# Gated attention and MLP on one core: strict program order on every engine, scores in groups of three, u turned a chunk after loading, and a new first batch

## The chip, the cores and the metric

One core of a Trainium2 chip runs the kernel. The metric is the device time of one execution in microseconds (us); lower is better. The kernel before takes 1306.66 us (median of 3 runs, 1306.63 to 1307.92).

## The reference

```python
def attn(u, v, z):                       # u, v: (8, 3008, 256), z: (8, 3008, 64)
    scores = (1.0 / S) * z @ z.transpose(0, 2, 1)
    return u * (np.maximum(scores, 0.0) ** 2 @ v)

def moe(x, w_in, w_out):                 # x: (24064, 256), w_in: (256, 2048), w_out: (2048, 256)
    h = x @ w_in
    return (h / (1.0 + np.exp(-1.702 * h))) @ w_out
# out = moe(attn(u, v, z).reshape(24064, 256), w_in, w_out)
```

Scores are symmetric, so the kernel computes only the upper half of the score blocks and gets the lower half by DMA transposes.

## The kernel before

A batch has 3008 rows, in six chunks of 512 (the last has 448). Each batch goes through attention (chunks 0 to 5), then up-projections (`up_group`, 48 of them, a tile `hg` each) and down-projections (`down`, halves of 128 rows, tile `yp`). Scores (`sc`) of a chunk pair are made in groups, ahead of their use; ScalarE rectifies (`rl`), VectorE squares (`a`), SyncE issues the DMA transposes (`tt`). The parts that matter:

```python
    ps2 = ctx.enter_context(tc.tile_pool(name="ps2", bufs=3, space=bass.MemoryType.PSUM))  # sc and hg share these
    ps1 = ctx.enter_context(tc.tile_pool(name="ps1", bufs=2, space=bass.MemoryType.PSUM))  # o and yp share these
    ctx.enter_context(tc.manual_schedule(engines={mybir.EngineType.PE}))  # the rest: ordered by a scheduler
    # ... cut ...
    def load_u(b, i):                    # 4 DMAs on SyncE's queue, then the transpose on VectorE
        # ... cut: uq <- u, two buffers ...
        dve.transpose(ut[...], uq[...])
    # ... cut ...
    def scores(b, group, dve_relu=False):
        # ... cut: two half-height matmuls for each sc ...
            act.activation(rl, sc, AF.Relu, scale=csc)
            dve.tensor_tensor(a, rl, rl, ALU.mult)
            # ... cut: one or two sp.dma_start_transpose(t, a) ...
    # ... cut ...
        def gate(c):                     # frees the accumulator acc[c]
            dve.tensor_tensor(x[:, c, :n], acc[c][:, :n], ut[:, :n], ALU.mult)
    # ... cut ...
    LEAD = {30: 2, 36: 2, 42: 2}         # score groups of the next batch among the up-projections
    TAIL = {2: 3, 5: 3}                  # and among the last down-projections
    # ... cut ...
    for b in range(B):
        for i in range(NCH):
            if i + 1 < NCH:
                load_u(b, i + 1)
            for n, step in enumerate(attend(b, i, both=(b == 0 and i == 0))):
                take(b, sched[i].get(n, 0))          # a score group
                if i == NCH - 1 and n % 5 == 2 and h < HEAD:
                    up_group(b, h); h += 1
                step()                               # a matmul of V with a
            if b == 0 and i == 1:
                # ... cut: pool.dma_start of W1 (4 DMAs) and W2 ...
        # ... cut: load_z, load_v, load_u of the next batch ...
        for q in range(HEAD, nup):
            take(b + 1, LEAD.get(q, 0))
            up_group(b, q)
            if q >= LAGY:
                down(b, *downs.pop(0))
        for n in range(len(downs)):
            take(b + 1, TAIL.get(n, 0), dve_relu=True)
            down(b, *downs[n])
```

Of the kernel before, what the change touches and what calls it, by code (L numbers as in the profile page):

```python
# [9 lines left out]
F32 = mybir.dt.float32  # L10
F16 = mybir.dt.float16
P = 128
# [3 lines left out]
def kernel(  # L16
# [51 lines left out]
    ctx.enter_context(tc.manual_schedule(engines={mybir.EngineType.PE}))  # L68

    ident = const.tile([P, P], F16, name="ident")  # L70
    make_identity(nc, ident)

    ZT, V16, UT, XT, unit, TT = {}, {}, {}, {}, {}, {}

    def warm_up(n):

        nil = const.tile([P, CH], F16, name="nil")
        dve.memset(nil, 0.0)
        w = ps1.tile([P, CH], F32, name="w", tag="ps1")
        for k in range(n):  # L80
            pe.matmul(w, nil[:, :P], nil, start=(k == 0), stop=(k == n - 1))

    def first_z(g):

        if g == 0:
            ZT[0] = pz.tile([P, NJ, P], F16, name="ZT", tag="ZT")
            ZT["st"] = pz.tile([P, NJ, 2, DQK], F16, name="zst", tag="zst")
        if g % CB == 0:
            ZT["f"] = pw.tile([P, CB, CB, DQK], F32, name="zf", tag="y")
        n0 = g * CB  # L90
        zf = ZT["f"][:, g % CB]
        full = min(CB, NJ - 1 - n0)
        sp.dma_start(zf[:, :full, :], z[0, n0 * P:(n0 + full) * P].rearrange("(n p) d -> p n d", p=P))
        if full < CB:
            for h in range(2):
                sp.dma_start(zf[h * SREM:(h + 1) * SREM, full, :], z[0, S0:S])
        z2 = ZT["st"][:, n0:n0 + CB]
        for c in range(2):
            dve.tensor_copy(z2[:, :, c, :], zf)
        return z2  # L100

    def first_zt(g, z2):
        zp = ps1.tile([P, CB, P], F16, name="zp", tag="ps1")
        for k in range(CB):
            pe.transpose(zp[:, k, :], z2[:, k, :, :], ident)
        act.activation(ZT[0][:, g * CB:(g + 1) * CB, :], zp, AF.Copy, scale=1.0)  # L106
# [14 lines left out]
    def load_v(b, eng):  # L121


        V16[b] = pz.tile([P, NJ, NCC, P], F16, name="V16", tag="V16")
        for n0 in range(0, NJ, VB):
            vst = pu.tile([P, VB, D], F32, name="vst", tag="vst", bufs=3)
            full = min(VB, NJ - 1 - n0)
            eng.dma_start(vst[:, :full, :], v[b, n0 * P:(n0 + full) * P].rearrange("(n p) c -> p n c", p=P))
            if full < VB:
                for h in range(2):  # L130
                    eng.dma_start(vst[h * SREM:(h + 1) * SREM, full, :], v[b, S0:S])
            for k in range(NCC):
                pool.tensor_copy(
                    V16[b][:, n0:n0 + VB, k, :].rearrange("p n (q c) -> p n q c", c=QW),
                    vst.rearrange("p n (q k c) -> p n q k c", k=NCC, c=QW)[:, :, :, k, :],
                )
# [4 lines left out]
    def load_u(b, i):  # L141
        n = width(i)
        uq = pu.tile([P, CH // QW, NCC, QW], F32, name="uq", tag="uq")
        src = u[b, i * CH:i * CH + n].rearrange("(q t) c -> t q c", t=QW)
        for k in range(P // QW):
            cs = slice(k * NCC * QW, (k + 1) * NCC * QW)
            sp.dma_start(uq[k * QW:(k + 1) * QW, :n // QW].rearrange("t q k c -> t q (k c)"), src[:, :, cs])  # L147
        ut = pu.tile([P, NCC, CH // QW, QW], F32, name="ut", tag="ut")
        UT[b, i] = ut
        dve.transpose(ut[:, :, :n // QW, :].rearrange("p k q t -> p q k t"), uq[:, :n // QW])  # L150


    def scores(b, group, dve_relu=False):
# [11 lines left out]
        for n, ((i, jp), sc) in enumerate(zip(group, scs)):  # L165
            rl = pw.tile([P, 2, CH], F16, name="rl", tag="rl", bufs=5)
            if dve_relu and n == 2:
                dve.tensor_scalar(rl, sc, 0.0, csc, ALU.max, ALU.mult)
            else:
                act.activation(rl, sc, AF.Relu, scale=csc)  # L170
            a = pa.tile([P, 2, CH], F16, name="a", tag="a", bufs=21)
            unit[b, i, jp] = a
            dve.tensor_tensor(a, rl, rl, ALU.mult)  # L173
            cj = jp // 2
            if cj > i:
                if (b, i, cj) not in TT:
                    TT[b, i, cj] = pa.tile([P, CB, CB, P], F16, name="tt", tag="tt", bufs=14)
                t = TT[b, i, cj]
                k0 = 2 * (jp % 2)
                if cj < NCH - 1:  # L180
                    sp.dma_start_transpose(
                        t[:, k0:k0 + 2].rearrange("p r g c -> p (r g) c"),
                        a.rearrange("p r c -> p (r c)"),
                    )
                else:
                    for r in range(2):
                        sp.dma_start_transpose(t[:, :, k0 + r, :], a[:, r, :])  # L187
# [12 lines left out]
    def attend(b, i, both=False):  # L200


        n = width(i)
        acc = {}

        def open_(c):
            if c not in acc:
                acc[c] = ps1.tile([P, CH], F32, name="o", tag="ps1")
                return True
            return False  # L210

        def mm(c, j):
            new = open_(c)
            last = c == 1 and j == NJ - 2 and not both
            pe.matmul(acc[c][:, :n], V16[b][:, j, c, :], weights(b, i, j), start=new, stop=last)  # L215
            if last:
                gate(c)

        def half():
            a = unit[b, i, NU - 1][:, 1, :n]  # L220
            for c in range(2):
                h = slice(c * SREM, (c + 1) * SREM)
                new = open_(c)
                pe.matmul(acc[c][:, :n], V16[b][h, NJ - 1, c, :], a[h], start=new, stop=not new)  # L224
            for c in range(2 if both else 1):
                gate(c)
# [13 lines left out]
        js = range(NJ - 1)  # L240
        if both:
            return [lambda j=j, c=c: mm(c, j) for j in js for c in range(2)] + [half]
        return [lambda j=j: mm(0, j) for j in js] + [half] + [lambda j=j: mm(1, j) for j in js]


# [27 lines left out]
    def down(b, k, s, h):  # L273
# [15 lines left out]
        if h == 1 and s == ns - 1:  # L289
            r0 = b * S + i * CH  # L290
            full = min(n, S - i * CH) // P
            act.dma_start(
                out[r0:r0 + full * P].rearrange("(n p) c -> p n c", p=P), Y[b, k][:, :full, :],
            )
            if full < ns:
                for h_, bb in enumerate((b, b - 1)):
                    act.dma_start(
                        out[bb * S + S0:(bb + 1) * S], Y[b, k][h_ * SREM:(h_ + 1) * SREM, full, :],
                    )


    LAGY = NFG + 1
    HEAD = 9

    def pieces(i):
        return [(i, jp) for jp in range(2 * i, NU)]

    def split(lst, sizes):
# [9 lines left out]

    LEAD = {30: 2, 36: 2, 42: 2}
    TAIL = {2: 3, 5: 3}  # L320
    SCHED = {
        0: {8: 3, 15: 2, 23: 3, 34: 2},
        1: {6: 3, 23: 3, 34: 2},
        2: {8: 3, 23: 3},
        3: {8: 2, 23: 2},
        4: {23: 2},
        5: {},
    }

    SCHED0 = {  # L330
        0: {0: 2, 8: 2, 16: 2, 24: 2, 32: 3, 40: 3},
        1: {0: 2, 8: 2, 15: 3, 23: 3, 34: 2},
        2: SCHED[2], 3: SCHED[3], 4: SCHED[4], 5: {},
# [4 lines left out]
    def take(b, n, **kw):  # L338
        if n:
            group = [queue.pop(0) for _ in range(n)]  # L340
            scores(b, group, **kw)
# [5 lines left out]
    warm_up(12)  # L347
    fill(0)
    z2 = [first_z(g) for g in range(NCH)]
    load_v(0, act)  # L350
    load_u(0, 0)
    first_zt(0, z2[0])
    take(0, 2)
    first_zt(1, z2[1])
    take(0, 2)
    for g in range(2, NCH):
        first_zt(g, z2[g])

    for b in range(B):
        nup = NCH * NFG  # L360
        sched = SCHED if b else SCHED0
        for i in range(NCH):
            if i + 1 < NCH:
                load_u(b, i + 1)
            h = 0
            for n, step in enumerate(attend(b, i, both=(b == 0 and i == 0))):
                take(b, sched[i].get(n, 0))
                if i == NCH - 1 and n % 5 == 2 and h < HEAD:
                    up_group(b, h)
                    h += 1  # L370
                step()
            if b == 0 and i == 1:
                w1v = moe_w_in.rearrange("(q k c) f -> q c k f", k=NCC, c=QW)
# [4 lines left out]
        if more:  # L378
            load_z(b + 1)
            load_v(b + 1, sp)  # L380
            load_u(b + 1, 0)
            fill(b + 1)
        downs = down_list(b)
        for q in range(HEAD, nup):
            if more:
                take(b + 1, LEAD.get(q, 0))
# [3 lines left out]
        for n in range(len(downs)):  # L390
            if more:
                take(b + 1, TAIL.get(n, 0), dve_relu=True)
# [31 lines left out]
```

## Time and profile before

| | before |
|---|---|
| time, median | 1306.66 us |
| span of the profiled run | 1304.2 us |
| TensorE busy | 96% |
| first relu; first V matmul | 15.26 us; 22.8 us |
| V matmuls of chunk 1 begin | 47.9 us |
| V matmuls of batch 1 begin | 200.5 us |

The last three rows are read from the timeline. Below is the top of the profile page of the kernel before: span, busy time, granted clock by fortieths of the span (in tenths of full speed), and the chain of waits that ended last. In the profile PE is TensorE, PEld its weight loads, DVE VectorE, ACT ScalarE, POOL GpSimd and SP SyncE; a q after the name is that engine's instruction queue, and L with a number a line of that run's own kernel.

```profile
span 1304.2 us, 19129 instructions
PE 1249.4 (96%) x7556; PEld 682.2 (52%) x7556; DVE 823.0 (63%) x899; ACT 748.7 (57%) x810; POOL 96.4 (7%) x149
PEclk7899999999999999999999999999999999999999
...
PE 88%; DMA 4%; DVE 3%; ACT 3%; issue 1%; SPq 1%; ACTq 0%; DVEq 0%
```

TensorE is the bottleneck; idle time of any other engine costs nothing until it makes TensorE wait. Next, the table of waits of the kernel before (who waited for whom: total us, times, longest).

```profile
DVE ut L150 <- DMA uq<-in_u_dram: 27.9, 5, 9.9
...
PE hg L259 <- DVE gt L268: 13.4, 14, 1.0
...
PE sc L160 <- ACT ZT L106: 9.9, 2, 9.2
...
PE o L215 <- DVE a L173: 7.6, 2, 6.4
...
PE hg L259 <- ACT rl L170: 6.3, 7, 0.9
```

The two `hg` lines are one stop of about 1 us for each of the 21 score groups among the up-projections. One of them in the timeline (start, length, engine, line, operation, count, idle time before and its releaser):

```profile
158.34 0.60 PE L160 MATMUL sc<-ZT 64*128 64x512 f16 x4
158.63 1.23 DVE L268 TENSOR_TENSOR gt<-hg,sg 128x1024 f16<-128x1024 f32 x1 [0.51 <-ACT sg L267]
158.77 1.94 ACT L170 ACTIVATE rl<-sc 128x1024 f16<-128x1024 f32 x2 [0.18 <-PE sc L160]
...
159.91 1.02 PE L259 MATMUL hg<-xt,W_58 128*128 128x512 f16 x4 [0.96 <-DVE gt L268]
```

Two score tiles and the previous `hg` hold all three two-bank PSUM buffers, so the next up-projection waits until the product `gt` has freed one.

### The profile page before, as it was taken

To read this page: it belongs to the slowest core of one execution; us is meant where nothing else is said; L and a number is where in the kernel's file an instruction comes from. 1 tells how busy PE (TensorE), PEld (TensorE's weight loads), DVE (VectorE), ACT (ScalarE), POOL (GpSimd) and SP (SyncE) were. 2 spreads that over 40 slices of the span, in tenths; PEclk is the share of its full clock that TensorE was granted. 3 is DMA by queue.
4 is the path that set the end of the run, shared out by engine and by line. 5 is a ranking of instruction groups with operands and counts; after the bars stand their busy time and mean duration, and the time that the engine had idled before them with its cause. 6 is when DMAs were issued, how large, how long until landed. Compare 5 with 4: busy or idle time off the path is not lost.

```text
span 1304.2 us, 19129 instructions
## 1 busy us (share of the span) xinstructions
PE 1249.4 (96%) x7556; PEld 682.2 (52%) x7556; DVE 823.0 (63%) x899; ACT 748.7 (57%) x810; POOL 96.4 (7%) x149
## 2 busy tenths in 40 slices
PE   5789999999999999999999999999999999999998
PEld 2235664456634566346653465544655456644566
DVE  3436767477754776657766577656776567664674
ACT  4525666356663676536765367644676446663564
POOL 5002000030000200012000120002100010000000
PEclk7899999999999999999999999999999999999999
DMA  9979348791387916894157842678437742285011
GB/s 198 161 148 197 85 116 158 149 173 46 81 166 135 167 34 113 148 149 134 50 119 152 128 136 63 124 146 126 133 66 142 135 113 54 65 160 109 1 49 49
DMA packets 476970, 152.53 MB, mean 117 GB/s; under 512 B 425937, under 2 KB 476625, under 8 KB 476881
## 3 DMA queue, kind: packets, MB, share of 16 engines
q1 hardware_dynamic: 402656, 115.93, 45.2%
q0 software_dynamic: 46064, 7.61, 7.7%
q10 hardware_dynamic: 28160, 27.79, 6.6%
q8 instruction: 59, 0.97, 0.3%
q14 instruction: 31, 0.25, 0.1%
HBM read 65.80 MB, written 24.64 MB: 69 GB/s over the span
## 4 chain that ended last, share of the span: by engine, by line
PE 88%; DMA 4%; DVE 3%; ACT 3%; issue 1%; SPq 1%; ACTq 0%; DVEq 0%
PE o L215 34%; PE hg L259 25%; PE yp L282 24%; PE sc L160 5%; DVE gt L268 1%; ACT sg L267 1%; DMA uq<-in_u_dram 1%; ACT rl L170 1%; DVE a L173 1%; DMA vst<-in_v_dram 1%; PE o L224 1%; DMA tt<-a 1%; DMA zf<-in_z_dram 1%; SPq L187 0%; SPq L147 0%
## 5 line engine op out<-in xcount | busy, mean ns | idle before, releaser
L268 DVE TENSOR_TENSOR gt<-hg,sg 128x1024 f16<-128x1024 f32 (+1 forms) x384 | 460.7, 1201 | 184.7 <-ACT sg L267 183.5
L267 ACT ACTIVATE sg<-hg 128x1024 f16<-128x1024 f32 (+1 forms) x384 | 386.4, 1006 | 266.4 <-PE hg L259 264.2
L170 ACT ACTIVATE rl<-sc 128x1024 f16<-128x1024 f32 x322 | 308.4, 1024 | 250.8 <-PE sc L160 232.4
L282 PE MATMUL yp<-W_59,gt 128*128 128x256 f16 x3008 | 381.8, 273 | 0.0
L259 PE MATMUL hg<-xt,W_58 128*128 128x512 f16 (+1 forms) x1408 | 354.5, 374 | 17.0 <-DVE gt L268 13.4
L282 PEld LDWEIGHTS <-gt 128*128 128x128 f16 x3008 | 293.2, 98 | 102.8 <-issue 5.9
L173 DVE TENSOR_TENSOR a<-rl 128x1024 f16<-128x1024 f16 x336 | 227.0, 690 | 120.3 <-ACT rl L170 119.8
L259 PEld LDWEIGHTS <-W_58 128*128 128x128 f16 x1536 | 150.1, 98 | 136.5 <-issue 28.2
L232 DVE TENSOR_TENSOR xt<-o,ut 128x512 f16<-128x512 f32 x80 | 54.9, 688 | 102.0 <-PE o L215 63.3
L160 PE MATMUL sc<-ZT 64*128 64x512 f16 x672 | 99.0, 385 | 12.5 <-ACT ZT L106 9.9
L150 DVE STREAM_TRANSPOSE ut<-uq 128x1024 f32<-128x1024 f32 (+1 forms) x48 | 58.6, 1221 | 35.5 <-DMA uq<-in_u_dram 27.9
L113 POOL DMA_DIRECT2D zst<-in_z_dram x14 | 21.3, 1524 | 732.3 <-DMA ZT<-zst 732.3
L288 ACT ACTIVATE y<-yp 128x512 f32<-128x512 f32 x96 | 56.1, 585 | 27.9 <-PE yp L282 24.5
L160 PEld LDWEIGHTS <-ZT 64*128 64x128 f16 x672 | 23.2, 94 | 72.2 <-issue 54.1
L215 PEld LDWEIGHTS <-V_124 128*128 128x128 f16 x276 | 26.3, 100 | 53.5 <-issue 23.7
L215 PE MATMUL o<-a,V_124 128*128 128x512 f16 (+1 forms) x156 | 38.7, 391 | 7.6 <-DVE a L173 7.6
L215 PEld LDWEIGHTS <-V_10392 128*128 128x128 f16 x276 | 25.9, 98 | 33.9 <-issue 5.3
L215 PEld LDWEIGHTS <-V_990 128*128 128x128 f16 x276 | 25.9, 98 | 33.9 <-issue 5.3
L215 PEld LDWEIGHTS <-V_4124 128*128 128x128 f16 x276 | 25.9, 98 | 33.9 <-issue 5.3
L215 PEld LDWEIGHTS <-V_7258 128*128 128x128 f16 x276 | 25.9, 98 | 33.9 <-issue 5.3
L215 PEld LDWEIGHTS <-V_5680 128*128 128x128 f16 x276 | 25.9, 98 | 33.7 <-issue 5.1
L215 PEld LDWEIGHTS <-V_2546 128*128 128x128 f16 x276 | 25.9, 98 | 33.7 <-issue 5.1
(63 smaller groups left out, 689.9 us busy)
## 6 DMA issues: line engine op xcount, KB each, us to landing
uq<-in_u_dram SPq DMA_DIRECT2D x160, 128.0 KB, 3.0
out_dram<-y ACTq DMA_DIRECT2D x40, 512.0 KB, 2.9
vst<-in_v_dram SPq DMA_DIRECT2D x35, 512.0 KB, 5.0
zst<-in_z_dram POOLq DMA_DIRECT2D x14, 368.0 KB, 8.1
tt<-a SPq DMA_TRANSPOSE x320, 3.2
uq<-in_u_dram SPq DMA_DIRECT2D x32, 112.0 KB, 2.6
out_dram<-y ACTq DMA_DIRECT2D x8, 384.0 KB, 3.8
vst<-in_v_dram SPq DMA_DIRECT2D x7, 384.0 KB, 5.6
```

Source lines behind the costliest of these rows:

```text
L113: pool.dma_start(zst[:, :NJ - 1, c, :], zd)
L150: dve.transpose(ut[:, :, :n // QW, :].rearrange("p k q t -> p q k t"), uq[:, :n // QW])
L160: pe.matmul(sc[:, r, :], zt[h, 2 * jp + r, :], zt[h, i * CB:(i + 1) * CB, :], start=True, stop=True,)
L170: act.activation(rl, sc, AF.Relu, scale=csc)
L173: dve.tensor_tensor(a, rl, rl, ALU.mult)
L215: pe.matmul(acc[c][:, :n], V16[b][:, j, c, :], weights(b, i, j), start=new, stop=last)
L232: dve.tensor_tensor(x[:, c, :n], acc[c][:, :n], ut[:, :n], ALU.mult)
L259: pe.matmul(hg[:, e, :n], W1[:, c, ff * P:(ff + 1) * P], XT[b, i][:, c, :n], start=(c == 0), stop=(c == NCC - 1),)
L267: act.activation(sg[:, :, :n], hg[:, :, :n], AF.Sigmoid, scale=1.702 / FSC)
L268: dve.tensor_tensor(g, hg[:, :, :n], sg[:, :, :n], ALU.mult)
L282: pe.matmul(yp[:, s % 2, :], GT[b, k, ff // CB][:, ff % CB, s * P:(s + 1) * P], W2[:, ff, :], start=(ff == 0), stop=(ff == NFF - 1),)
L288: act.activation(Y[b, k][:, s0:s + 1, :], yp[:, :s % 2 + 1, :], AF.Copy, scale=1.0 / FSC)
```

## The change

Its intent: take the score groups out of the up-projections, so that they no longer compete for those buffers; make every engine's order explicit; keep the weight loads out of the start (the program of the kernel before has them after chunk 1 too, but its scheduler issued them at 1.3 to 27.5 us); have u landed before VectorE turns it. Besides, the third rectification of a group among the down-projections goes from VectorE (`dve_relu`) to ScalarE.

```diff
-    ctx.enter_context(tc.manual_schedule(engines={mybir.EngineType.PE}))
+    ctx.enter_context(tc.manual_schedule(engines={ET.PE, ET.Pool, ET.SP, ET.DVE, ET.Activation}))
@@ u: the transpose is split off
-        dve.transpose(ut[...], uq[...])          # at the end of load_u
+    def turn_u(b, i):
+        dve.transpose(ut[...], UQ.pop((b, i))[...])
@@ output: the very last block goes out in two parts; head start of the up-projections
-    LAGY = NFG + 1
-    HEAD = 9
+    LAGY = 2 * NFG + 3
+    HEAD = {NCH - 2: (14, 4), NCH - 1: (0, 4)}
@@ score groups
-    LEAD = {30: 2, 36: 2, 42: 2}
-    TAIL = {2: 3, 5: 3}
+    TAIL = {3: 3, 7: 3, 11: 3, 15: 3}
-        0: {8: 3, 15: 2, 23: 3, 34: 2},
-        1: {6: 3, 23: 3, 34: 2},
-        # ... cut ...
+        0: {4: 3, 15: 3, 26: 3, 37: 3},
+        1: {8: 3, 23: 3},
+        # ... cut: 14 groups of three a batch in all ...
@@ first batch: z in four loads, cast by VectorE as it lands; V by pieces from two queues (cut)
@@ attention
-            if i + 1 < NCH:
-                load_u(b, i + 1)
+                if n == 12:
+                    if b == 0 and i < 2:
+                        turn_u(b, i)
+                    if (b or i) and i + 1 < NCH:
+                        turn_u(b, i + 1)
+                    if i + 2 < NCH:
+                        load_u(b, i + 2)
@@ weights: not before the gate of chunk 1
             if b == 0 and i == 1:
+                hold = const.tile([P, 1], F16, name="hold")
+                pool.tensor_copy(hold, XT[b, i][:, 0, :1])
                 # ... cut: the loads of W1 and W2; the next batch's z follows them on GpSimd's queue ...
```

## The prediction

> **What bounds it now.** TensorE is busy 96% of the span (page, busy shares) and is 88% of the chain of waits; VectorE 63%, ScalarE 57%. In the timeline steady matmuls start 216 ns (512 columns) or 109 ns (256) apart. Summed over all matmuls (half-height pairs overlapping) that is about 1203 us; some 95 us are lost between matmuls, 5.5 us follow the last. The losses:
>
> 1. Start, to the end of the first chunk at 47 us: 26 us. ScalarE stands in its DMA queue behind V loads waiting for staging buffers, so the first score is rectified at 15.3 us instead of 8; TensorE waits 9.2 us for ZT. Later a u transpose stands in VectorE ahead of the squares, waiting 10 us for u behind weight loads hoisted to the start; TensorE stops 6.4 us. The clock record drops to half after each stop.
> 2. Rest of the first batch: about 15 us, mostly VectorE and SyncE waiting for u (chain of waits), and another half-clock stretch.
> 3. Three score groups of two among the up-projections, in seven batches: the next up-projection finds all three two-bank PSUM buffers taken. Table of waits: hg waits 13.4 us for the gelu product and 6.3 us for the relu: 19.7 us.
> 4. Each switch between half-height score matmuls and full ones: 95 ns in, 92 ns out, 17 groups a batch.
>
> **What the change does.** The large matmuls stay.
> - Groups of three sit only in attention and among the last down-projections, which use no two-bank buffer: cause 3 vanishes, -20 us. 14 groups instead of 17, several placed next to the half-height remainder pair and sharing its switch: -4 us. After odd batches three output DMA issues (2.2 us of ScalarE's queue) precede relus: +3 us.
> - Nineteen up-projections go into the last two attention chunks (nine before): 0.
> - u is turned a chunk after loading, so VectorE finds it landed. After attention, V then u of the next batch should land 10 us in; the transpose stands 14 us in (8 pairs of 1.74 us): no stall.
> - Start: ScalarE issues only three V loads, interleaved; weights wait for chunk 1; VectorE copies most of transposed z. I expect the first attention matmul near 10 us and chunk 0 ending near 30 us, limited by z landing, VectorE and a half-clock stretch: -16 us. Rest of the batch: -11 us.
> - Split last output DMA: -0.5 us. Smaller stalls: -2 us.
>
> **Predicted time: 1255 us, 8 in 10 between 1246 and 1270.** Chances: over 2% faster 0.94, within 2% 0.04, slower 0.02.
>
> **What would show each step right.** In the table of waits hg no longer waits for the gelu product or relu; TensorE's idle total falls from about 55 us to under 20; the first relu starts near 8 us; the clock record has one half-clock stretch after warm-up (the Trainium skill, "TensorE: Matmul & The Clock Gate", Part 1: an idle window of about 3.4 us halves the clock; the trace's 13.7 us half-clock stretch around the 9 us stop agrees). A steady batch loses under 4.5 us between matmuls, against 7 to 8.9 now.
>
> **What would make it wrong.** Strict order: if u of the next batch lands after its transpose's turn, every gelu product behind it waits, several us in each of seven batches. SyncE issues transposes at 1.3 us each; a backlog in chunks 0 to 2 would delay u and the first batch's squares. Groups of three 2.4 us apart in chunk 0 leave ScalarE (0.95 us per relu) almost no slack, so TensorE may wait for PSUM there.

## The result, and the profile after

The changed kernel takes 1293.11 us (median of 4, 1291.99 to 1294.89), the kernel before 1307.29 us (median of 4 in the same comparison). The ratio is 0.9892 (95% interval 0.9874 to 0.9909): 14 us faster, where 51 were predicted. Ratios are the mean time of one kernel's runs over that of the other's of the same rounds, so not quite the ratio of the medians. The page of the kernel after, the lines that answer to those above:

```profile
span 1291.9 us, 19134 instructions
PE 1249.0 (97%) x7555; PEld 684.0 (53%) x7555; DVE 804.2 (62%) x890; ACT 758.1 (59%) x819; POOL 97.2 (8%) x150
PEclk9969999999999999999999999999999999999999
...
PE 89%; SPq 3%; DMA 3%; DVE 2%; issue 1%; ACT 1%; ACTq 0%; DVEq 0%
```

The start is better: the lowered digits at the beginning (7 and 8, means over slices with half-clock stretches in them) are gone. A new one (the 6) stands in the third slice, 65 to 97 us. The table of waits of the kernel after:

```profile
DVE ut L163 <- DMA uq<-in_u_dram: 92.1, 15, 18.2
...
PE o L234 <- DVE xt L243: 25.4, 9, 12.5
...
PE o L234 <- DMA tt<-a: 6.6, 2, 5.4
...
PE sc L173 <- ACT rl L180: 3.2, 7, 0.5
```

No `hg` line is left: that stop is gone. In its place, VectorE waits 92.1 us for u, three times as long as before, and TensorE waits 25.4 us for the gate (`xt`) that VectorE had not got to. Where the time went, by the first V matmuls of chunk 1 and of batch 1 (from the timeline), in us; "expected" sets the terms of the prediction on the three stretches:

| stretch | before | expected change | after | change |
|---|---|---|---|---|
| start to chunk 1 | 47.9 | -16 | 27.8 | -20.1 |
| chunk 1 to batch 1 | 152.6 | about -14 | 171.7 | +19.1 |
| batch 1 to the end | 1103.7 | about -21 | 1092.4 | -11.3 |

So the start gained more than expected. The rest of the first batch lost 33 us against what was expected, and the steady batches about 10.

**The first batch.** The windows of the kernel before (length; busy time and instructions of TensorE, its weight loads, VectorE, ScalarE, GpSimd; granted clock; mean busy share of the 16 DMA engines, which comes out above 1 at times, so it is read only against other windows; GB/s):

```profile
0.00:30.00 30.00, 16.65 (x76) 6.48 (x77) 10.67 (x22) 12.95 (x16) 14.24 (x26) 0.77 0.89 198
55.00:75.00 20.00, 17.42 (x88) 6.68 (x86) 10.56 (x16) 10.65 (x12) 0.00 (x0) 1.00 0.88 152
```

The same windows of the kernel after:

```profile
0.00:30.00 30.00, 26.66 (x125) 9.37 (x127) 19.75 (x37) 17.39 (x18) 9.20 (x18) 1.00 1.07 214
55.00:75.00 20.00, 5.36 (x17) 1.67 (x14) 6.03 (x9) 1.45 (x2) 0.00 (x0) 0.65 1.61 157
```

Between 55 and 75 us TensorE does 17 matmuls instead of 88, at 0.65 of its clock, while the DMA share is nearly twice as high. The bytes moved in a second are nearly the same (157 GB/s against 152): each byte kept the DMA engines busy longer. VectorE's timeline there, after:

```profile
48.34 0.69 DVE L183 TENSOR_TENSOR a<-rl 128x1024 f16<-128x1024 f16 x1 [0.22 <-ACT rl L180]
65.61 1.25 DVE L163 STREAM_TRANSPOSE ut<-uq 128x1024 f32<-128x1024 f32 x1 [16.57 <-DMA uq<-in_u_dram]
66.78 1.85 DVE L183 TENSOR_TENSOR a<-rl 128x1024 f16<-128x1024 f16 x3
68.55 0.68 DVE L243 TENSOR_TENSOR xt<-o,ut 128x512 f16<-128x512 f32 x1
```

and TensorE's:

```profile
53.81 2.98 PE L234 MATMUL o<-a,V_97 128*128 128x512 f16 x13
69.28 3.57 PE L234 MATMUL o<-tt,V_97 128*128 128x512 f16 x8 [12.50 <-DVE xt L243]
78.29 1.89 PE L234 MATMUL o<-tt,V_97 128*128 128x512 f16 x4 [5.44 <-DMA tt<-a]
```

The u transpose for chunk 3 stands in VectorE's queue ahead of three squares and a gate of chunk 2. Its data lands at 65.5 us; behind it all wait, the accumulator is not freed, and TensorE stops for 12.5 us. The DMA issues of 42 to 75 us after (size of one, median us to landing) say why u was late:

```profile
W_58<-in_moe_w_in_dram POOLq DMA_DIRECT2D x4, 256.0 KB, 9.0
W_59<-in_moe_w_out_dram POOLq DMA_DIRECT2D x1, 1024.0 KB, 18.8
zst<-in_z_dram POOLq DMA_DIRECT2D x2, 368.0 KB, 24.8
uq<-in_u_dram SPq DMA_DIRECT2D x4, 128.0 KB, 15.8
tt<-a SPq DMA_TRANSPOSE x10, 6.9
```

Over the whole run the medians are 3.6 us for u and 3.2 us for a transpose. SyncE itself is held up too, in its timeline (start, length, operation, count):

```profile
39.83 5.48 SPq L191 DMA_TRANSPOSE tt<-a  x4
45.41 11.25 SPq L156 DMA_DIRECT2D uq<-in_u_dram  x4
56.76 8.81 SPq L191 DMA_TRANSPOSE tt<-a  x2
```

Its issues of that u took from 45.41 to 56.66 us, against 2.2 us for four at other times, so the transposes behind them start late. It had also come to them late: it issued transposes from 29 to 45.4 us without a pause.

**The steady batches.** Adding up the starts of all matmuls against their steady pace, TensorE loses 3.6 us in an undisturbed batch, as expected. In batches 1, 3, 5 and 7 it loses 1.4 to 2.7 us more at one gate that stands behind a late u transpose (of chunk 3; the waits of VectorE for u are for chunks 3 and 4 in every batch), and at the start of batches 2, 4 and 6 about 1.3 us for PSUM.

### The profile page after: what moved, and what is told of

Same layout as the page of the kernel before. It is cut to its first block, busy times and chain, and to the rows that moved or that the text cites. A ratio compares the mean times of both kernels' runs of the same rounds, so it can differ in the third digit from the quotient of the medians.

```text
span 1291.9 us, 19134 instructions
## 1 busy us (share of the span) xinstructions
PE 1249.0 (97%) x7555; PEld 684.0 (53%) x7555; DVE 804.2 (62%) x890; ACT 758.1 (59%) x819; POOL 97.2 (8%) x150
## 4 chain that ended last, share of the span: by engine, by line
PE 89%; SPq 3%; DMA 3%; DVE 2%; issue 1%; ACT 1%; ACTq 0%; DVEq 0%
PE o L234 33%; PE yp L290 25%; PE hg L267 25%; PE sc L173 6%; DMA uq<-in_u_dram 2%; SPq L191 1%; SPq L156 1%; DVE a L183 1%; ACT rl L180 1%; SPq L197 1%; DVE xt L243 0%; DMA zf<-in_z_dram 0%; DMA tt<-a 0%; ACTq L308 0%; PE zp L110 0%
## 5 line engine op out<-in xcount | busy, mean ns | idle before, releaser
L180 ACT ACTIVATE rl<-sc 128x1024 f16<-128x1024 f32 x336 | 320.0, 1025 | 242.4 <-PE sc L173 221.6
L290 PE MATMUL yp<-W_59,gt 128*128 128x256 f16 x3008 | 371.1, 273 | 0.0
L290 PEld LDWEIGHTS <-gt 128*128 128x128 f16 x3008 | 292.0, 98 | 91.4 <-issue 11.9
L267 PEld LDWEIGHTS <-W_58 128*128 128x128 f16 x1536 | 149.6, 98 | 125.9 <-issue 1.6
L163 DVE STREAM_TRANSPOSE ut<-uq 128x1024 f32<-128x1024 f32 (+1 forms) x48 | 58.3, 1216 | 92.1 <-DMA uq<-in_u_dram 92.1
L173 PE MATMUL sc<-ZT 64*128 64x512 f16 x672 | 95.7, 385 | 3.2 <-ACT rl L180 3.2
L234 PEld LDWEIGHTS <-V_97 128*128 128x128 f16 (+1 forms) x288 | 27.0, 102 | 65.7 <-issue 33.5
L234 PE MATMUL o<-tt,V_97 128*128 128x512 f16 (+1 forms) x120 | 33.2, 412 | 24.1 <-DVE xt L243 17.5
L234 PEld LDWEIGHTS <-V_10477 128*128 128x128 f16 (+1 forms) x288 | 27.1, 99 | 38.1 <-issue 8.8
L234 PEld LDWEIGHTS <-V_1075 128*128 128x128 f16 (+1 forms) x288 | 26.8, 98 | 37.0 <-issue 6.8
L234 PEld LDWEIGHTS <-V_4209 128*128 128x128 f16 (+1 forms) x288 | 26.7, 98 | 36.2 <-issue 6.4
L234 PEld LDWEIGHTS <-V_7343 128*128 128x128 f16 (+1 forms) x288 | 26.8, 98 | 35.7 <-issue 5.5
L234 PEld LDWEIGHTS <-V_5765 128*128 128x128 f16 (+1 forms) x288 | 26.8, 98 | 34.3 <-issue 4.4
L234 PEld LDWEIGHTS <-V_2631 128*128 128x128 f16 (+1 forms) x288 | 26.8, 98 | 34.3 <-issue 4.4
L234 PEld LDWEIGHTS <-V_8899 128*128 128x128 f16 (+1 forms) x288 | 26.8, 98 | 34.3 <-issue 4.4
```

Source lines behind the costliest of these rows:

```text
L163: dve.transpose(ut[:, :, :n // QW, :].rearrange("p k q t -> p q k t"), UQ.pop((b, i))[:, :n // QW])
L173: pe.matmul(sc[:, r, :], zt[h, 2 * jp + r, :], zt[h, i * CB:(i + 1) * CB, :], start=True, stop=True,)
L234: pe.matmul(acc[c][:, :n], V16[b][h, j, c, :], a[h], start=k == first[c], stop=k == final[c])
L267: pe.matmul(hg[:, e, :n], W1[:, c, ff * P:(ff + 1) * P], XT[b, i][:, c, :n], start=(c == 0), stop=(c == NCC - 1),)
L290: pe.matmul(yp[:, s % 2, :], GT[b, k, ff // CB][:, ff % CB, s * P:(s + 1) * P], W2[:, ff, :], start=(ff == 0), stop=(ff == NFF - 1),)
```

## The experiments

Theories. **A**: the weights and the next batch's z, issued together on GpSimd's queue at 43 us, crowd u and the transposes on the shared DMA engines. The Trainium skill ("DMA: Bandwidth & Descriptors", Issuing engines are not separate DMA queues) says that DMAs of all issuing engines run on the same 16 DMA engines and interleave; the landing times above agree. **B**, the rival: SyncE's own queue, with transposes at about 1.27 us an issue, makes u late whatever else is under way. **C**: strict order on VectorE turns a late u into a stop, because squares and gates stand behind it. (The same skill, "TensorE: Matmul & The Clock Gate", Architectural detail: ScalarE and VectorE queues are strictly first in, first out. VectorE's timeline above agrees: idle 16.57 us with squares behind.) In all experiments the rest of the kernel is the changed one. "Stretch 2" is chunk 1 to batch 1 in the profiled run; it is 171.7 us in the changed kernel.

### No weight loads (w_none)

```diff
-    # the hold and the loads of W1 and W2
+    pool.memset(W1, 0.0)
+    pool.memset(W2, 0.0)      # at the start; the result is wrong on purpose
```

> The changed kernel with both weight matrices set to zero on GpSimd at the start instead of loaded (wrong result on purpose): 4 MB of reads less after chunk 1. Theory A (the weights and the next batch's z, issued together at 43 us, fill the DMA engines, and u of chunks 3 and 4 and the transposes land late): the stops of 12.7 and 5.9 us in chunks 2 and 3 of the first batch vanish or shrink under 3 us, and the half-clock stretch with them; time about 1272 us, 20 under the changed kernel. Rival B (SyncE's own queue of transposes at 1.3 us each makes u late, whatever else is on the DMA engines): u of chunk 3 is still late, gain under 5 us.

Measured 1281.90 us (ratio 0.9811). The gain is 11 us, between the two expectations. Stretch 2 fell to 159.3 us. The longest wait for a gate fell to 5.6 us, but eight waits remain: without the hold, the next batch's z moved up to 25 us and met the first transposes. The run also started 3 us later. So A is part of it and the run is not clean; `no_w` below repeats it better.

The late start was the experiment's own doing: GpSimd's two memsets ran from 1.3 to 8.2 us, and a cast of z on VectorE that started at 4.6 us took 3.71 us, where it took 0.30 us in the changed kernel and in `no_w`, whose memsets came at 22 us.

The longest of its stops speaks for B as well. VectorE's wait for chunk 4's u, SyncE's issues of it and TensorE's stop:

```profile
75.94 2.17 SPq L156 DMA_DIRECT2D uq<-in_u_dram  x4
80.92 1.25 DVE L163 STREAM_TRANSPOSE ut<-uq 128x1024 f32<-128x1024 f32 x1 [13.23 <-DMA uq<-in_u_dram]
84.59 3.49 PE L234 MATMUL o<-tt,V 128*128 128x512 f16 x8 [5.64 <-DVE xt L243]
```

From 56 to 84 us only SyncE's own transfers were under way, landing in the usual 3.1 us (u) and 3.0 us (transposes), and SyncE issued without a pause: u was late because of its place in that queue. This is not B alone, though: z had held the same queue up before (four transposes took 9.8 us to issue from 33.5 us on, against 5.5).

### Weights earlier (w_early)

```diff
+    # the loads of W1 and W2, before the batch loop: right after the V casts on GpSimd
     ...
             if b == 0 and i == 1:
                 # the hold stays, now only in front of the next batch's z
-                # loads of W1 and W2
```

> The changed kernel with the weight loads issued right after the first batch's V casts (about 23 us) instead of after chunk 1; the hold stays in front of the next batch's z. Theory A: the congestion moves to 23 to 43 us, where u of chunk 2 and chunk 0's transposes are under way; the 12.7 us stop goes, smaller ones may come: 1273 to 1288 us. Rival B: no change within 3 us.

Measured 1295.34 us, correct (0.9903): a miss on the slow side. Stretch 2 is 171.4 us, unchanged: now five stops of 2.4 to 7.9 us, from 27, 43, 53, 77 and 91 us on, instead of three. Moving the traffic into another crowded time gains nothing.

### The u transpose later (turn_late)

```diff
                 if n == 12:
-                    if b == 0 and i < 2:
+                    if b == 0 and i == 0:
                         turn_u(b, i)
-                    if (b or i) and i + 1 < NCH:
-                        turn_u(b, i + 1)
                     if i + 2 < NCH:
                         load_u(b, i + 2)
+                if n == 40 and i + 1 < NCH:
+                    turn_u(b, i + 1)
```

> The changed kernel with the u transpose for the next chunk at step 40 of a chunk instead of step 12, so that squares and gates stand before it in VectorE's queue; loads and weights as they were. Theory C (strict order is what turns a late u into a stop: squares and the gate wait behind the transpose): u lands as late as before, but the 12.7 us stop falls under 4 us, the stops of 1.4 to 2.8 us in batches 1, 3, 5 and 7 (8.5 us in all) vanish; the 5.9 us stop for a DMA-transposed tile stays; 1270 to 1280 us. If only lateness of DMA counts (A or B without C), the gain is under 5 us, the wait just moves to step 40 or to the next gate.

Measured 1276.95 us, correct (0.9772). The waits of TensorE and, below, of VectorE:

```profile
PE o L234 <- DMA tt<-a: 17.8, 1, 17.8
...
PE o L234 <- DVE xt L243: 3.2, 3, 1.5
```

```profile
DVE ut L163 <- DMA uq<-in_u_dram: 2.6, 2, 1.6
```

One placement in VectorE's queue takes its wait for u from 92.1 to 2.6 us. From batch 1 to the end the span is 1082.4 us against 1092.4: the 10 us missing in the steady batches are this. Theory C holds there, and the expected stretch of about 1083 is reached. In the first batch the 12.5 us stop is gone, but the transposed tile that TensorE then needs is late in turn: a stop of 17.8 us, where I had expected 5.9 to stay. The late DMA was only hidden behind the late gate: 17.8 us is what the stops of 12.5 and 5.4 us came to before. Stretch 2 fell to 163.2 us, partly because the later stop of 4.1 us went too.

### The u load earlier (u_early)

```diff
+                turn_u(b + 1, 0)          # in the up-projections, as before
+                load_u(b + 1, 2)
     ...
-                    if i + 2 < NCH:
-                        load_u(b, i + 2)
+                    if i + 3 < NCH:
+                        load_u(b, i + 3)  # right after turn_u(b, i + 1); chunk 0 of batch 0 alike
```

> The changed kernel with each u load one chunk earlier in SyncE's queue (two buffers still, each refilled as soon as it has been turned), weights as they were. Theory B for the steady batches (u stands behind transposes in SyncE's queue): the stops of 1.4 to 2.8 us in batches 1, 3, 5, 7 vanish, -8 us. First batch: u of chunks 3 and 4 is issued before the weights, so the 12.7 and 4.3 us stops go, but the transposes still meet the weights: the 5.9 us stop for a transposed tile stays. About 1268 us, 1262 to 1278.

Measured 1283.35 us, correct (0.9816): worse than expected. The steady part is right: batch 1 to the end takes 1082.2 us, so the late u there came from its place behind transposes in SyncE's queue (B). The first batch is not: TensorE waits 22.8 us for transposed tiles, 12.9 and 10.0 us long. Stretch 2 is 168.5 us.

### The next batch's z later (z_late)

On top of the late turn; `held(i)` is the same one-element copy, of chunk i's gate.

```diff
+            if b == 0:
+                held(4)
             load_z(b + 1)
```

> The run with the u transpose at step 40, and the next batch's z held back until the gate of chunk 4 instead of following the weights. Its one large stop (17.8 us for a transposed tile in chunk 3, while weights and z were landing between 45 and 77 us) should shrink if z's two small-row loads share the blame (theory A): to 8 to 13 us, total 1268 to 1273 us. If SyncE's own pace of 1.3 us a transpose makes the tile late (rival B), the stop stays within 2 us and the time at 1277.

Measured 1272.49 us, correct (0.9739), as theory A expected: the stop fell from 17.8 to 10.9 us.

### The second weight matrix later as well (w_split)

```diff
             if b == 0 and i == 1:
                 # hold, loads of W1
-                # load of W2
+            if b == 0 and i == 3:
+                held(3)
+                # load of W2
```

> As the run before, and the second weight matrix held until the gate of chunk 3; only the first matrix follows chunk 1. Theory A: only 4 loads meet the transposes, the stop in chunk 3 falls to 2 to 7 us: 1260 to 1267 us. Rival B: 1277 us as with the late turn alone.

Measured 1269.86 us, correct (0.9717; 1267.12 to 1274.16): above what was expected. The stop in chunk 3 is 8.4 us, and 2.6 us appeared where W2 meets the transposes. No gain over `z_late` is shown: the times of the two overlap, stretch 2 is 158.2 us against 158.6, and such a stop varies from run to run (`out_pool` below, the same program until 188 us, has 11.9 us there).

### Score groups back among the up-projections (lead_back)

On top of the late turn.

```diff
-    TAIL = {3: 3, 7: 3, 11: 3, 15: 3}
+    LEAD = {30: 2, 36: 2, 42: 2}
+    TAIL = {3: 3, 11: 3}
     ...
+                take(b + 1, LEAD.get(q, 0))
             up_group(b, q)
```

> The run with the u transpose at step 40, but with three score groups of two back among the up-projections at the pairs 30, 36 and 42, as in the kernel before, and two of three among the last down-projections. If those groups cost what the table of waits said (about 1 us each, 21 of them), plus one more switch a batch, the time is 1277 + 20 to 24 = about 1299 us, and hg waits about 20 us again. If the down-projections were no better a place, it stays within 5 us of 1277.

Measured 1297.79 us, correct (0.9926): 20.8 us over the late turn alone (1276.95). TensorE's waits:

```profile
PE hg L267 <- ACT rl L180: 12.6, 14, 0.9
PE hg L267 <- DVE gt L276: 4.8, 7, 1.0
```

The stop is back, 17.4 us in 21 times. Of the other 3.4 us, 1.4 is a longer stop in chunk 3 of this run (19.2 us against 17.8); one more group's switches a batch would be about 1.3 us, by an estimate from 0.19 us each. This part of the change is worth what was predicted.

### Only TensorE in program order (sched_free)

```diff
-    ...manual_schedule(engines={ET.PE, ET.Pool, ET.SP, ET.DVE, ET.Activation})
+    ...manual_schedule(engines={ET.PE})
```

> The changed kernel with only TensorE in program order, the other engines ordered by the scheduler as in the kernel before. If strict order (theory C) rather than DMA lateness is what costs, this recovers most of the 8.5 us in the steady batches and part of the first batch: 1270 to 1283 us. If the scheduler, which does not know that u is late, places the u transposes no better, 1288 to 1300 us.

Measured 1278.00 us, correct (0.9781): the same change without strict order is 15 us faster than with it. From batch 1 to the end it takes 1082.1 us, as with the late turn. It is not a test of order alone: the scheduler also issued the weights at 1.3 to 24 us, which cost the start (TensorE waits 6.4 us for ZT, chunk 1 begins at 36.6 us instead of 27.8).

### Transposes that only chunk 5 needs put off (defer)

On top of `w_split`, first batch only.

```diff
+                if b == 0 and cj == NCH - 1 and i < 3:
+                    later.append((b, i, jp, a))     # issued in chunks 2 and 3
+                else:
+                    turned(b, i, jp, a)             # issues the transposes, as before
```

> The run with the split weights, and in the first batch the transposes that only chunk 5 needs (two issues a score pair) put off to chunks 2 and 3, so that those for chunk 3 come about 10 us sooner in SyncE's queue. Theory B for what is left (SyncE's queue, 1.3 us a transpose, and blocked while the first matrix lands): the 8.4 us stop in chunk 3 falls under 2 us: 1260 to 1264 us. If only the DMA engines' load counts (A), the stop stays above 5 us and the time above 1266.

Measured 1263.39 us, correct (0.9678; 1261.57 to 1270.85). The stop in chunk 3 fell from 8.4 to 1.3 us, as B expected of what was left; the first matrix still followed chunk 1. In the profiled run, which was the slowest of the four, a 6.1 us stop at the start of chunk 4 appeared behind W2, so that stretch 2 (158.1 us) is no shorter than in `w_split`; the two fastest runs took 1261.6 us. The times of both kernels overlap, so the gain of 6 us in the median is less sure than the shorter stop in chunk 3.

### The first matrix earlier (w1_early)

```diff
+    # loads of W1 before the batch loop, right after the V casts; on top of w_split
```

> The run with the split weights, and the first matrix issued right after the first V casts (about 23 us) instead of after chunk 1. Theory A: the 8.4 us stop moves to chunk 1 or 2 and is not smaller than 4 us in sum, since the transposes already fill the DMA queue there: 1264 to 1272 us. If the window from 20 to 43 us had room, 1259 to 1262 us.

Measured 1274.49 us, correct (0.9753): a little above the range under theory A. The stops for tiles add up to 12.3 us against 11.0 in `w_split`, a difference within what such stops vary by.

### Outputs of the last chunk from GpSimd's queue (out_pool)

```diff
-            act.dma_start(out[...], Y[...])
+            (pool if k == NCH - 1 and b < B - 1 else act).dma_start(out[...], Y[...])   # on top of w_split
```

> The run with the split weights, and the output of each batch's last chunk issued from GpSimd's queue instead of ScalarE's. If ScalarE's three issues (about 2.2 us) are what keeps the score groups of chunk 0 waiting for PSUM after odd batches, those stops of 1.4 to 1.6 us in batches 2, 4 and 6 go: 4 us less, 1264 to 1267 us. If groups of three 2.4 us apart are too dense by themselves, the time stays at 1270.

Measured 1283.32 us, correct (0.9823): 13 us slower than `w_split` instead of 4 faster. The waits of TensorE for the relu (3.4 us in `w_split`) did vanish, so ScalarE's issues were their cause. But GpSimd's queue is in program order too: the z of the batch after next stands behind these outputs, and so moved from a quiet time into chunk 0. The issues of 345 to 365 us in this run:

```profile
zst<-in_z_dram POOLq DMA_DIRECT2D x2, 368.0 KB, 9.9
uq<-in_u_dram SPq DMA_DIRECT2D x4, 128.0 KB, 8.9
...
tt<-a SPq DMA_TRANSPOSE x9, 5.8
```

and of 343 to 363 us, the same place, in `w_split`:

```profile
uq<-in_u_dram SPq DMA_DIRECT2D x4, 128.0 KB, 3.5
tt<-a SPq DMA_TRANSPOSE x13, 3.3
```

This is theory A again, in a steady batch and without weights.

### No weights, cleanly (no_w)

Both matrices set to zero on GpSimd during chunk 0, no loads (wrong result), z where `defer` has it. The edit also holds the late outputs of `out_late` below, which the expectation doesn't mention: the run stands on top of `out_late`, and about 4 us of its gain over `defer` are those outputs'.

> The run with put-off transposes, and both weight matrices set to zero on GpSimd during chunk 0 instead of loaded (wrong result on purpose). Theory A: what the first batch still loses after chunk 0 (about 18 us, of it 10 us in stops for transposed tiles and 3 us at chunk starts) is the weights' doing: no stop over 2 us left after chunk 1, time 1250 to 1254 us, within a few us of what was predicted. Rival B (SyncE's transposes by themselves too slow for this order): stops of 5 us or more stay, 1258 us or more.

Measured 1251.91 us (0.9578). The same windows as above, in this run:

```profile
0.00:30.00 30.00, 24.37 (x119) 8.63 (x120) 20.67 (x38) 17.28 (x18) 15.75 (x20) 1.00 1.05 213
55.00:75.00 20.00, 20.00 (x101) 8.53 (x99) 10.69 (x15) 9.29 (x11) 0.00 (x0) 1.00 0.75 141
```

TensorE is busy throughout the second window and the DMA share is 0.75 instead of 1.61; stretch 2 is 143.1 us. With the order of the other transfers mended, the weights' traffic is all that is left of the first batch's stops: A. The time lies in A's range only with the help of the late outputs; the missing stops do not depend on them.

### Outputs issued later (out_late)

On top of `defer`: the outputs of a batch's last chunk stay on ScalarE, but are issued at the start of the next batch's chunk 1.

> The run with put-off transposes, and the outputs of each batch's last chunk issued by ScalarE at the start of the next batch's chunk 1 instead of right after its last copy. The stops of 1.1 to 1.6 us after batches 1, 3 and 5 go, nothing moves on GpSimd's queue: 4 us less than 1263, about 1259 us. If the run with GpSimd's queue was slow for another reason than its order, these stops stay.

Measured 1259.88 us, correct (0.9644; 1259.71 to 1261.87), the fastest correct version: 3.6% under the kernel before. Its page, and the longest wait of TensorE:

```profile
PE 1239.7 (99%) x7555; PEld 681.8 (54%) x7555; DVE 809.9 (64%) x890; ACT 758.0 (60%) x819; POOL 97.2 (8%) x152
```

```profile
PE o L248 <- DMA tt<-a: 4.2, 1, 4.2
```

The relu wait is gone, and every steady batch now loses 3.6 to 3.8 us: batch 1 to the end takes 1077.9 us, against 1082.1 in `defer`. Stretch 2 is 150.9 us.

### The second matrix last (w2_last)

On top of `out_late`: W2 held until chunk 4's gate, with z right behind it.

> The run before, and the second weight matrix held until chunk 4's gate (with the next batch's z right behind it). Theory A: the 6.3 us stop at the start of chunk 4 goes, but the matrix now meets the transposes for chunk 5 and z: between 3 us faster and 3 us slower than the run before. If it is over 5 us faster, there was room for it.

Measured 1261.94 us, correct (0.9654): 2 us slower, within the expectation. The stop moves and stays. The 8 us between `out_late` and `no_w` (stretch 2: 150.9 and 143.1 us) are what the weights still cost; no placement tried hides them.

## Why the prediction was wrong

The direction was right; the size was not: -14 us instead of -51.

- **"cause 3 vanishes, -20 us": right.** `lead_back` puts it back and pays 20.8 us; the `hg` waits are gone from the table after.
- **"After odd batches three output DMA issues ... +3 us": right.** `out_late` takes those stops away, and batch 1 to the end falls by 4.2 us.
- **"chunk 0 ending near 30 us ... -16 us": right, somewhat better.** Chunk 1 begins at 27.8 us, -20.1; the first relu starts at 8.39 us and the first V matmul at 11.4 us. The half-clock stretch that was expected there did not come (granted clock 1.00 from 0 to 30 us).
- **"weights wait for chunk 1 ... Rest of the batch: -11 us": wrong, the largest error.** The stretch grew by 19.1 us. I took away the cost of the weights where they had been and charged none where they went. There they met z, u and the transposes, on a SyncE queue that already ran without a pause at 1.27 us a transpose. With z moved away TensorE's stop in chunk 3 fell from 17.8 to 10.9 us, with W2 moved too it was 8.4, with the chunk 5 transposes put off in SyncE's queue 1.3, and without weights no stop over 1.5 us was left after chunk 1 began. So it is not the weights alone. In stretch 2, 171.7 us in the changed kernel, taking the loads away without mending the order leaves 159.3 (`w_none`, in which z also came early), mending the order and the times of issue with the loads kept leaves 150.9 (`out_late`), and both together 143.1 (`no_w`): without any weights, the order and the time of the next z are still worth 16 us.
- **"u is turned a chunk after loading, so VectorE finds it landed": wrong.** A chunk later in TensorE's order is not a chunk later in SyncE's. SyncE reaches the load only after the transposes before it, and VectorE waited 92.1 us for u. Under strict order squares and gates stood behind the transpose. That cost 10 us in the steady batches (`turn_late`, `u_early` and `sched_free` all recover it). In the first batch it made the 12.5 us stop, but most of that returned as a wait for a tile when the transpose moved. My list of dangers named SyncE's backlog, but only for the first batch, and I gave it no time in the sum. The danger it named for the steady batches, the next batch's u, did not come true: that transpose never waited; the late ones were those of chunks 3 and 4.
- **"several placed next to the half-height remainder pair ... -4 us": agrees, not isolated.** An undisturbed batch loses 3.6 us, under the 4.5 predicted.
- **"TensorE's idle total falls from about 55 us to under 20": wrong.** It was 43 us in the changed kernel; in `out_late` it is 18.
- **"one half-clock stretch": wrong.** Up to the last matmul the clock record has three, of 20.5, 6.8 and 3.4 us, each in a stop. The Trainium skill ("TensorE: Matmul & The Clock Gate", Part 1) has the clock halve after an idle window of about 3.4 us. The first agrees: TensorE did nothing in the 3.4 us before it. The other two don't: TensorE was busy for 0.90 and 1.21 us of the 3.4 us before the clock fell.

With the two wrong terms mended, the kernel comes to 1263.39 us (`defer`), 8 us over the 1255 predicted. The 1259.88 us of `out_late` need the late outputs besides, which the prediction had counted as a cost.

What stays open: how the first batch's loss divides between the weights and SyncE's backlog when both are present, since `w_none` moved z as well and `out_late` moved W2 and z; the runs show that the backlog is enough for late u's without weights (the steady batches, which `u_early` mends by order alone), and that the weights still cost 8 us with the order mended (`out_late` against `no_w`).

## What to carry to other kernels

A transfer moved out of one crowded time must be costed where it lands: look at the DMA share there and at what is waiting to land. When every engine runs in strict program order, ask of each instruction that waits for a DMA what stands behind it, and place it as late as its use allows; "a chunk earlier" counts in the issuing queue's time, not in TensorE's. Moving an issue to an idle engine's queue also moves everything behind it on that queue.

## What the Trainium skill lacked or had wrong

- "DMA: Bandwidth & Descriptors", Issuing engines are not separate DMA queues: it has the sharing right but no size for it. Here a 128 KB load of u went from 3.6 to 15.8 us and a transpose from 3.2 to 6.9 us to land, beside 2.9 MB of weights and z on GpSimd's queue (42 to 75 us).
- The same page: it has sequencer cycles for DMA transposes of other sizes, in a passage on trn3, but no time on the issuing queue for one like these. Here it was 1.27 us from one issue to the next at SyncE (128x1024 or half of it, fp16), and one issue took 6.2 us while the weights were landing; a plain issue of u took 0.49 us in the median and 6.7 us at most.
- "TensorE: Matmul & The Clock Gate", Part 1: the window before the clock halves need not be idle throughout. In the changed kernel the clock fell at 91.9 and 1170.5 us with TensorE busy for 0.90 and 1.21 us of the 3.4 us before; the second stop was only 2.41 us long, shorter than the idle window. A stop of 2.56 us (237.0 to 239.6 us) left the clock at full speed.
- "TensorEngine Tiling (Array Packing)", Key Properties: no time for a change of tiling mode, there or on the other pages looked through. Here a switch from full to half-height matmuls cost 96 ns (312 ns instead of 216 from one start to the next) and one back 92 ns (308).
